# Block-sparse attention with a gated convolution FFN: the sixth head pair's queries and keys are transposed by the DMA crossbar instead of TensorE, with a new instruction order

## The chip, the cores and the metric

The kernel runs on one core of a Trainium2 chip. A core has TensorE (matrix products, results in PSUM), VectorE and ScalarE (elementwise work), GpSimd (here it only issues loads and writes a few constants) and SyncE, called SP here (it only issues transfers). All transfers, whoever issues them, are carried by the same 16 DMA engines. The metric is the device time of one execution in microseconds (us); lower is better. Views of the trace give times from the start of the span, which runs from the first to the last instruction of the profiled execution.

## What is computed

Attention over 4 batches of 8 heads, 768 positions and 64 dimensions per head, with a mask in blocks of 32 positions, followed by a feed-forward block with a gate from a convolution of three taps:

```python
scores = (1.0 / np.sqrt(D)) * np.matmul(q, k.transpose(0, 1, 3, 2))
# mask: neighbouring blocks, first and last block of rows and columns, 3 sampled blocks per block row
scores = np.where(mask, scores, -1000000000.0)
attn = softmax(scores)                       # over the last axis
x = np.matmul(attn, v)                       # heads put side by side: (4, 768, 512)
h = np.maximum(x @ w_in, 0.0)                # (4, 768, 1024)
conv_out[s] = sum over k of conv_w[k] * h[s + k - 1]
out = (h * sigmoid(conv_out)) @ w_out        # (4, 768, 512)
```

Inputs and output are float32; the kernel works in bf16 with float32 accumulation.

## The kernel before

**Head pairs.** Two heads make a pair, so there are 16 pairs, numbered 0 to 15, four to a batch; the sixth is pair 5, in the second batch. A pair's queries and keys must lie with the 64 dimensions on partitions for the score products. They do so in a slot `t` of 24 tiles of 128 columns (five slots are used in turn): tiles 0 to 11 hold queries, 12 to 23 keys, and rows 64 to 87 hold the mask, which is added by the same product because the contraction runs over 88 rows.

**Two ways to fill a slot.** `kq_transposes` (L416) is used for pairs below `NPE`. GpSimd loads keys (192 KB) and the first half's queries (96 KB) into `nat`, with a cast to bf16. TensorE transposes them in blocks of 128x128 into a `mix` bank of PSUM: `k_tr` (L458) takes six transposes, `q_half` (L521) three for each half of the queries. VectorE or ScalarE copies the result into the slot: two copies of 64x768 for keys, two of 64x384 for each half of the queries (L331 on VectorE and L327 on ScalarE are the helper that records all such copies). The second half's queries come later, by a load of their own into `nq`. `kq_crossbar` (L552) is used for the pairs from `NPE` on. GpSimd loads keys and, outside the last batch, the queries of both halves in one load of 192 KB. SP issues two DMA transposes (L596), keys then queries, from `nat` into the staging tile `stg`. Two copies of 64x1536 (`stg_cp`, L602) then fill the slot, each waiting for both transposes. For the first five of these pairs SP also issues `m_turn` (L591), a 72 KB copy that lays the mask rows in the order that the crossbar's layout needs.

**Units.** Scores are computed in 144 units of eight 128x128 blocks. A unit is two groups of score products into an `st` tile (L755, `s`), one exponential on ScalarE over 128x1024 (L767, `exp`), and 8 products with the values (L792, `av`). Work goes through segments: the first or second half of the queries of one batch, 18 units each; the last half is cut in two segments of 12 and 6 units. Pair 5 is first needed in unit 40, and its second queries in unit 58.

**The feed-forward part** of a segment runs beside the next segments' attention. VectorE normalizes a pair's result (L702, `norm`). The result is turned so that features lie on partitions: by TensorE for the first and the last two segments, otherwise by a DMA transpose from SP (L711, `x_xb`). Then come the products with `w_in` (L889, `f1`), evictions of `hE` with the rectifier (L909 on ScalarE or L911 on VectorE, `relu`), the convolution on VectorE (L947, L955), tanh on ScalarE (L994), the gate on VectorE (L997, L1002), the products with `w_out` (L824, `f2`), the eviction of the output (L327 or L331, `ev`) and the store (L833).

**The order.** All operations are recorded in a graph of some 1,800 operations and then written out as the text `ORDER` says: two characters name an operation, a letter (V or A) after them its engine where there is a choice, and a digit the buffer that it takes. Each engine executes its own operations in this order, so the text sets the queue of every engine, GpSimd and SP included. Tile's dependency tracking adds the waits. Loads on GpSimd's queue are spaced by `pace`, a copy of one element that waits until an earlier load has landed (L666) or until a certain unit's exponential is done (L407); `SEQ` and `AHEAD` name the loads that are spaced by the first kind and how far apart.

Of the kernel before, what the change touches and what calls it, by code (L numbers as in the profile page):

```python
# [25 lines left out]
1ZV6s16t2sV25U16c4Z1s6u16d2W6x06y6h6i06q2H04U6z06j22bV6C16D2cV6r6v6k6w6E56L05VV6M1m6A6B6l06N36Q16mV6R6F2GV16G6S0
6H06V06I6W6O16P6X46J06T6+16KV6/2Iid17037301b1l74ig0ih7511pie7b1ifV157ciiA3237g07d26U7hiB16Y1x6Zij1iC7i4ik71iD7l1
727miEilAb2o07q07n07riFim1762qVin7s57827y12pV337zioV7707e7f7A3797j7D07EiJ27a22v04V1v7F1iK7k7o7p7I12wV44W7t3907u
iG3502xV2y17J7N04+7O522zV7K04S2J04T2AV3017B17C2KV07G2Zip17P54PiM7S14R1y7Tiq2LV7U47H7+02X1irVi7v07/7L7MiH7Q8017R
8317w847ViL2M17x8527W08802OV89is0iN7X18a381itiI18d1iuV8286iO8e8l02NV87iR08b8c8f5iy08miS36iv17Y8n18q1iU8riz8giP  # L30
8s07Z8v02UV08wiAV8h8o18p8x3iQiw8t1q8A13428BixAcjb08C48F03aV3iT8GiZ38u8y8zj518H5iV8N1i+jciWi/8O8S08i28Dj08P28Tj6
8j3o28E8IiX8U18k8X1j1538Y8J08Q2+V8R8Z08V3e900512/V3U08W91j2iY9812B28+1o9238/99j74Xj34/3l2jdj49a59d03c38K19e31V2
je37V9f1939i13k3bj83x18LjfA39jj9V28M19n0502P19o9k2jk038V949b14919cjl9p49509s1963p2C19t2EV9g9h9u39A03X02DV9BjmV
jh13nji3mV49C13g13d9F1jjV9Gjq09H59ljF09K09L97jG9mjr9M0jH9q9P19QjIja9R29rjn1jJjo3f39vjsV9w09X0jK9YjpV3w3s09D3q9E
a019x29Z39IjN3a19Jjw1jOjxa249ya50a6jQ9N9Oa752Q0jyVaa19S9TjP9+1ab2SAjt19U12RVac1jujR9/af09VjSa3aga43hjvVjC0a8jL
an1ah2a9jTaojV1adaejD9Wap3jMas0atjXaijz1au1jWax1ayjEVaj03taqarjAaz0jYak0aC0jUavaDjBAawjZ9zaAaBaK1aE2k12aLkf0k2j+
kr1k3aP0aQalaM03A2aFkgk4am2ks3IaR13zk53YaU1aGaN1j/aVk6aO3r4aZ0k03L4aaSa+aW4aTkh3D0k73C3J2ktaH1k8a/2b213M3b3aXki
b413jV3iVba0ku3E1kjA2aYbbaIkvV0b0bf1bc33ZkJ01rb1bg3Okx13Bbh2b5bk03vVbl3Nb60bdbm4kybe3uVbp1bikzV00bq3P0kK3Tbr1b72
bx0b8bykM13yV0kNkLA3aJbC1bjkOVbDbz2bnbol91bsbtkA0bu0bE5kBbvbH0bIkCVkG1bJ4lbkH3FbA0labM1bBbNkIAlcbFbR0bO2bS3QkV0
bGkD0kWkEbT5bKkXbLbZ1b9kYkFAdb+kS1bPbQb/1kT3KV13VV3c20l12jgc3bUldkkkl0kUAc40l3c71bwc8kP13HV4B3kQc943GVbV1c0cc0  # L40
4y1c1l2c5lecdck14bkZc6clce3cakm3RV1knl4kRA4cbcp0cm5bW13SVcqkolh3k91400kpA2lj45ka4n2cr1bXcu1cfkb3Wlf4Ck+likccg3/
cn03+kdA3cvk/lE0cw2l5coke4k0lFlH1lkl014e1cz04clGAcAl6cE1ch0cs4DlgctcxlK0bY0cB0llcy48lL4ol7cFlMVlIcG5cCcM0l8cNcD
lJVlB041cO1lCcicR1m50cSlDAlv1m6kwcT3cW0cXlZ2cHcI1lwl+cY44pcPm8cQcUc/1m7d0lmlp04lV2lxm9d104M0d70lqlnlomad84jcVm0
4d4Ed93dc1lrmbcJ2cZdd462c+mclsde24qlyl/d2d3ltV3lzA1dh0didm1cKlAlQ1dndj4d41cLm1da0lRdo0d5lN04mdr0lSVlOkqm2dbdslPV
dz1lT1ludt14fmd0dAdfdgmedklUdB2mfdllW0cjm3lXmglVAdE0dFm4lYAdpdJ1dG4dqdKmhd6mz1duml1dL0mAmmdO0dw2mnmidv1dCdPmodD
dHdIdMdQ5dW1mjmt0mpmumkmq4x4YdNdX42V244dRdSdY3mBd/0mr47V4e0mvdT0mse11e41dUe5mCe65dZ14Ae90mDV14reamweb443Vee1mR1
mxV24s0mSefdxeg2em0d+e24gV3mU0mVmTV194Fe3e7mWAe8ecener1nd1mX1eo1neesedmYnfet5ehm+04hVm/ew0ej14G1ngmZVfexn0Aei0
eB1eCey0epnl0eqeuev4teknnn11eD4na04Ln2nmeJ0n3AaeKdy2noeL1eO1ezeAeEnhePeFnbnpdVeQ5n41ncVeM1eT0n5nieUmEn6Vn70eV4eN
n84Hnt3njeY1eZeRnunqn9AjmF1e+2el4uV4eSf10mGnweG2eWf2nB2mL0myf35eHmMmH4inv4vAeXmNeIf90fanxfb3e/mInk0mOfe1nDf0mJA3
ffnrnCnEfj0mPV2f4fg0mKfkf50o21nsmQo3ny4zV3n/04wo4Vfo1fl2o0nFfpfcfd4NV1fho1AfinJ1f60nzfq1nKop1fw0nAnP0nGoqfxfB1fC  # L50
fy4nHfmfnornLnIfrfD3fsfG0osfHnMfI0otft1nQnNV2nRounSfufL04IV0nTA3fMnV1fN14JVfQ1nUnWf7nY0nXAnZovf81fz1owfRn+AfAo81
fS4oh0fY0fZfvoio50o9f+5ojo6okg11nOg2o7AoaVfEg60g32fFoloe0g7ox1fJfKomfOozoffPoyg80fTfU0gb1onf/ob1oAocogAfV0gcoo
odAgj0gkoBgd1g0g4g5oF2oT0oGoN1gl3g9go1oIgpoCgaoHoOfWgq5oJgeoUfXgfgm1oDgngt0oKgugg1oEgC1gDgrgv2gsoLoMoPoVgE5ghgw
gH0oWgigIoXA1oQgM1gJ1oRV0p304KgNp4gO3oSp5oYp6gxgV0p7A3gy1pc1gzgWg+1p90gX2papdpbV0bg/peAgF1gGh30h05px2gKh4gA1gLpz
pf0gPgBA0pygQgY0h51pggR0pApi1pjphA6pBhc1pkAhdgSgZh1pChh0pF3gT0pl1pGhe2h2h6h7gUVpmh82pHhipnA3po0hm1hj0h9pDhnpppE1
# [57 lines left out]
def kernel(  # L113
# [70 lines left out]
    A = sb.tile([MR, NB], FP32, tag="A", name="A")  # L184
# [684 lines left out]
    for n, (b, g, tok, C, _) in enumerate(SEGS):  # L869
# [4 lines left out]
        w1 = 128 * C  # L874
# [176 lines left out]
```

## Time and profile before

| | before |
|---|---|
| time, median of 3 runs | 207.29 us (207.22 to 207.52) |
| the profiled execution's own time | 207.06 us |
| its span, first to last instruction | 205.2 us |
| granted TensorE clock | 1.00 |
| transfers | 25.40 MB, mean 124 GB/s |

The profile's page gives for each engine the time in which it was busy and the share of the span, then the chain of work that ended last, then groups of equal instructions. In a group's row stand the line of the code, the engine (PE is TensorE matmul, PEld its weight load, DVE is VectorE, ACT is ScalarE, POOL is GpSimd, SP is SyncE), the tiles written and read, shapes, the count, the total busy time and the mean duration of one in ns, and the idle time of the engine before them with what ended it. Busy time of TensorE comes from modelled ends, so a full TensorE is not a TensorE at its peak.

### The profile page before, as it was taken

What the parts mean: (1) busy time and instruction counts of PE and PEld (TensorE: products, weight loads), DVE (VectorE), ACT (ScalarE), POOL (GpSimd) and SP (SyncE); (2) the same over time, 40 slices, a digit from 0 to 9 for tenths busy, and PEclk for the clock granted to TensorE, in tenths of its full rate; (3) what the DMA queues carried; (4) which work ended last, traced back from release to release, by engine and by line L of the source; (5) the groups of instructions that cost most, each with busy time, mean ns of one, the idle gap of its engine ahead of it and who ended that gap; (6) DMA issues with size and microseconds to landing.
All of it is one profiled execution on the core that took longest, in us unless ns stands there. A gap on an engine that the chain in (4) does not pass through costs nothing.

```text
span 205.2 us, 6186 instructions
## 1 busy us (share of the span) xinstructions
PE 198.2 (97%) x2398; PEld 142.9 (70%) x2417; DVE 184.4 (90%) x561; ACT 190.8 (93%) x251; POOL 60.8 (30%) x125
## 2 busy tenths in 40 slices
PE   7899999999999999999999999999999999999992
PEld 5688878876677776776666767766667667787760
DVE  6899889999999999899999999999999839999961
ACT  6999999999999999899999998999999989998931
POOL 8696652900890149021927011000000000000000
PEclk9999999999999999999999999999999999999999
DMA  6999999997599979999998911655122040011205
GB/s 150 151 176 166 152 188 198 152 220 106 78 154 198 195 105 118 201 103 219 150 177 135 255 30 38 80 134 170 33 72 73 19 132 2 3 51 56 102 3 204
DMA packets 51113, 25.40 MB, mean 124 GB/s; under 512 B 36780, under 2 KB 48140, under 8 KB 51084
## 3 DMA queue, kind: packets, MB, share of 16 engines
q0 software_dynamic: 20000, 11.24, 43.7%
q1 hardware_dynamic: 30796, 13.46, 32.5%
q8 instruction: 19, 0.31, 0.7%
q10 hardware_dynamic: 288, 0.30, 0.4%
q14 instruction: 10, 0.08, 0.2%
HBM read 23.09 MB, written 6.29 MB: 143 GB/s over the span
## 4 chain that ended last, share of the span: by engine, by line
PE 61%; ACT 20%; DVE 14%; issue 4%; ACTq 0%
PE st L755 20%; PE mix L824 15%; ACT pt L767 13%; PE mix L889 10%; PE av L792 10%; DVE m L947 4%; DVE t L331 3%; ACT hE L909 3%; DVE m L955 2%; PE av L229 2%; ACT m L994 2%; ACT t L327 1%; DVE hE L911 1%; DVE xtok L702 1%; PE st L824 1%
## 5 line engine op out<-in xcount | busy, mean ns | idle before, releaser
L767 ACT ACTIVATE pt<-st 128x1024 bf16<-128x1024 f32 (+1 forms) x145 | 142.2, 1041 | 2.6 <-PE st L755 1.4
L755 PE MATMUL st<-t 88*128 88x256 bf16 (+2 forms) x600 | 92.7, 267 | 1.1 <-ACT pt L767 0.4
L792 PEld LDWEIGHTS <-pt 128*128 128x128 bf16 x1152 | 56.2, 97 | 15.1 <-ACT pt L767 0.5
L792 PE MATMUL av<-vt,pt 128*128 128x65 bf16 x1152 | 63.5, 193 | 0.1
L755 PEld LDWEIGHTS <-t 88*128 88x128 bf16 x600 | 48.0, 97 | 20.6 <-issue 2.1
L889 PE MATMUL mix<-xT,winb 128*128 128x384 bf16 (+2 forms) x288 | 55.3, 307 | 0.1
L947 DVE TENSOR_SCALAR m<-hE,cw 128x382 bf16<-128x382 bf16 (+2 forms) x192 | 49.0, 314 | 0.9 <-ACT hE L909 0.5
L824 PE MATMUL mix<-woutb,gT 128*128 128x512 bf16 x165 | 46.5, 379 | 0.6
L955 DVE TENSOR_TENSOR m<-m 128x764 bf16<-128x764 bf16 (+2 forms) x64 | 33.7, 532 | 0.4
L889 PEld LDWEIGHTS <-winb 128*128 128x128 bf16 x288 | 23.5, 97 | 7.5 <-issue 0.5
L994 ACT ACTIVATE m<-m 128x764 bf16<-128x764 bf16 (+2 forms) x32 | 27.1, 847 | 0.0
L824 PEld LDWEIGHTS <-gT 128*128 128x128 bf16 x208 | 17.3, 97 | 9.5 <-DVE gT L1002 0.2
L909 ACT ACTIVATE hE<-mix 128x384 bf16<-128x384 f32 (+2 forms) x38 | 19.4, 527 | 0.6 <-PE mix L889 0.3
L702 DVE TENSOR_TENSOR xtok<-av,rcp 128x384 bf16<-128x384 f32 (+2 forms) x36 | 18.2, 505 | 0.4
L1002 DVE TENSOR_TENSOR gT<-m,hE 128x764 bf16<-128x764 bf16 (+3 forms) x36 | 18.0, 505 | 0.3
L238 POOL DMA_DIRECT2D nat<-in_q_dram x23 | 17.1, 746 | 3.7 <-DMA winb<-in_moe_w_in_dram 2.4
L407 POOL COPY pace<-pt 1x1 bf16<-1x1 bf16 x24 | 6.4, 268 | 38.1 <-ACT pt L767 37.8
L911 DVE TENSOR_SCALAR hE<-mix 128x384 bf16<-128x384 f32 x26 | 14.3, 553 | 3.1 <-PE mix L889 2.8
L238 POOL DMA_DIRECT2D nat<-in_k_dram x15 | 10.9, 726 | 16.2 <-DMA stg<-nat 14.1
L238 POOL DMA_DIRECT2D vn<-in_v_dram x16 | 11.9, 746 | 6.8 <-DVE vt L331 5.1
L331 DVE COPY t<-mix 64x384 bf16<-64x384 bf16 (+1 forms) x30 | 12.3, 416 | 0.7 <-ACT t L327 0.2
L997 DVE TENSOR_SCALAR m<-m 128x764 bf16<-128x764 bf16 (+3 forms) x36 | 11.8, 332 | 0.8 <-ACT m L971 0.2
(80 smaller groups left out, 121.4 us busy)
## 6 DMA issues: line engine op xcount, KB each, us to landing
out_dram<-o2s SPq DMA_DIRECT2D x23, 256.0 KB, 3.3
vn<-in_v_dram POOLq DMA_DIRECT2D x16, 192.0 KB, 5.4
nat<-in_k_dram POOLq DMA_DIRECT2D x15, 192.0 KB, 5.2
nat<-in_q_dram POOLq DMA_DIRECT2D x6, 192.0 KB, 6.1
winb<-in_moe_w_in_dram POOLq DMA_DIRECT2D x2, 512.0 KB, 11.0
woutb<-in_moe_w_out_dram POOLq DMA_DIRECT2D x4, 256.0 KB, 8.2
nat<-in_q_dram POOLq DMA_DIRECT2D x9, 96.0 KB, 5.1
nq<-in_q_dram POOLq DMA_DIRECT2D x6, 96.0 KB, 4.8
```

The costliest lines, as they stand in the source:

```text
L238: return op(name, {eng: occ}, lambda e: on(e).dma_start(out=dst(), in_=src), prio, deps, dma=(kind, service), **kw)
L331: nc.vector.tensor_copy(out=dst, in_=src)
L702: nm = op("norm", {"DVE": t_dps(128 * C)}, lambda e: nc.vector.tensor_tensor(out=xtok_t[xk.index][:, 0:C].rearrange("p c h d -> p h c d"), ...
L755: nc.tensor.matmul(out=st[:, 128 * x:128 * (x + n_)], lhsT=t[0:88, 12 + 6 * hh + kc, :], rhs=t[0:88, idx:idx + (n_ - 1) * (2 if P < NPE el ...
L767: nc.scalar.activation(out=pt_t[ptb.index][:, c0:c1], in_=st_t[stb.index][:, c0:c1], func=AF.Exp, bias=0.0, scale=0.125)
L792: nc.tensor.matmul(out=o[:, off:off + 65], lhsT=pt_t[ptb.index][:, 128 * x:128 * x + 128], rhs=V_t[vslot_b[P].index][:, hh, kc, 0:65], sta ...
L824: nc.tensor.matmul(out=acc(), lhsT=gT_t[gb.index][:, ffc, 128 * t:128 * t + 128], rhs=woutb[:, ffc, c0:c1], start=(ffc == 0), stop=(ffc == ...
L889: nc.tensor.matmul(out=mix_t[hb.index][:, w1 * y:w1 * y + w1], lhsT=winb[:, fc, 128 * ffc:128 * ffc + 128], rhs=xT_t[xt_buf[n].index][:, f ...
L909: nc.scalar.activation(out=dst, in_=src, func=AF.Relu, bias=0.0, scale=0.5)
L947: nc.vector.tensor_scalar(out=m_t[cb.index][:, x, y, 0:w], in0=hE_t[heb.index][:, f0 + y, t0 + x:t0 + x + w], scalar1=cw[:, x, f0 + y:f0 + ...
L955: nc.vector.tensor_tensor(out=m[:, a_, :, 0:w], in0=m[:, a_, :, 0:w], in1=m[:, b_, :, 0:w], op=ALU.add)
L994: th = [op("tanh", {"ACT": t_act(2 * w) + 0.04}, lambda e, cb=cb, w=w: nc.scalar.activation(out=m_t[cb.index][:, 0, :, 0:w], in_=m_t[cb.in ...
```

## The change

`NPE` goes from 6 to 5, so pair 5 is filled by `kq_crossbar` instead of `kq_transposes`. Its keys and queries go through a staging tile; its queries of both halves come in one load; its separate load of second-half queries (`nq5`) leaves the sequence of spaced loads. As the mask copy `m_turn` is made for the first five crossbar pairs, it is now made for pairs 5 to 9 instead of 6 to 10. Score products of pair 5 read the slot in the crossbar's layout. The whole `ORDER` is a different one, from its first line on: positions on every queue, the engine of operations that have a choice, and buffer numbers.

```diff
 ORDER = """
-0M0L001c0R010210N0S0O031h041d1i0V1g0P051P3060Q0712V081e0W090a0T11A0b1f1N00c0d0U0e16A1Q1z00X1F11AA02d21H00Y1GA0f
...
+0M0L000R010210T0N0S0O030W040P050V061N00Q070812V091P10a11A0U0b0c0d1Q0e16A1z10X2130f1F01AA01H00Y1GA1g0g0h0i0/V0+A
...
-    NF, NPE = 4, 6
+    NF, NPE = 4, 5
     WHOLE = ()
-    SEQ = "nq0 nq1 nq2 k4 q4 nq3 v4 k5 q5 w0 v5 w1 k6 q6 w2 w3 v6 k7 q7 v7 nq4 nq5"
+    SEQ = "nq0 nq1 nq2 k4 q4 nq3 v4 k5 q5 w0 v5 w1 k6 q6 w2 w3 v6 k7 q7 v7 nq4"
     AHEAD = 4
```

Counted from the two texts, the operations whose number on an engine differs are these (the transposes and copies of pair 5 among them):

| operation | before | after |
|---|---|---|
| `hE` evictions on ScalarE / VectorE | 38 / 26 | 33 / 31 |
| output evictions on ScalarE / VectorE | 15 / 11 | 17 / 9 |
| staged copies on ScalarE / VectorE | 1 / 19 | 0 / 22 |
| copies of keys from PSUM on ScalarE / VectorE | 3 / 11 | 2 / 10 |
| copies of queries from PSUM on ScalarE / VectorE | 3 / 21 | 4 / 16 |
| copies of turned results on ScalarE / VectorE | 5 / 7 | 4 / 8 |
| transposes of keys / queries on TensorE (groups) | 7 / 13 | 6 / 11 |
| crossbar transposes of queries and keys | 20 | 22 |
| loads of second-half queries, spaced | 2 | 1 |
| pace copies | 42 | 41 |

More of the change, by code (lines that the diff above doesn't have):

```diff
@@ L26 @@
[L26 to L55, printed above, removed]
@@ new lines @@
+6P2X26C16Q26T16DV6M4J6U1li616V1i71x1v146Y06Zi8V01i906+3741ia2GV1ibV756N6R7646Siu26W7907aiw2o06X7b26/7e17012L2qV
+7127f2pVic1iv7g0id7j02T0ieVf7k77if07l5ix7r17s72ig7t1iy787317w07cihV2v14X7diz2O17h2wV47i7x2J07m2xV7y32Z07n7B17C
+iC17u0ii12R2y07D47o07v7G02zV7H1y7p7zij7I52AV7L14L4Q7MiA4N7AikVail07N07T0iD7Uim2MV7V17E7Y1inV7Z7F7J7K7+37O810iEiF
+827P17W7Q18352NV86187iGiB1ir03018827X8e0isiK38fiHio1iL2S17/8j17R808g484858kitV89ipiM8l02U8a8o0iqV88p8h0iN8q18t1
+iI8u8i1p8m8n8v54W2+8y0iOj418b28r2B22PV0iP8s8ziJ8w8G136iS08A38H341i+08c8x4P8I1iT8d8L08MiQj5iViU8N08B8Q12/28Ri/2WV
@@ new lines @@
+8S28C1398V0iW318J8W2VV8KiX8O8P8TiR8U9118X4927qiYj6iZj09338D29608E977Sj1j71o9853f4T2YV39b1j2V29c3g28F2j8A18Y8Z940
+9d09532V9g09h992C033V3a39a9i29e3i9l18+03722DVjd18/9m2EAje4Y3D09n4909t0jfV9uja03j035V2jb9v39y1jcV9zjj19A59fjy19D0
+9EjAjg09F09jjz9I13b0389JjhjB9K19k4Mjk4IjiV9o9Q09q19RjlA3hV49p19w3rjC9S29V19x9WjG09Bjp19r9X49C3n13k9G9+0jHjq3s29/
+jDjrVa31a49sjm0jJa059H9LjI9M9T09U9YjEa50jn3cjK3ua809ZjoVa1a2jLa99N0ag1jO2ah3m4a6aa49Ojs1a7jv0jP9Pai2jFal0amjMjw
+jRan0ab3oaq13xad23larjQac1ajakas5jNjtaoaeav0awjuAjxVaf0aD1ax2apjSaEkk1jW0ataF1aujXaI03C3v3k80jYaJjTayazjZaG0kl
@@ new lines @@
+cu1cl4fV0cx1lBkV1cmk/cq48144lzVcycF0lccrcz0cGlD0l0cvlEkplCVcH24icwcAkdlecK1cLkj42l1li1lFAcccB1cC2cM3cP0cIl+3cJ
+lu045l9cQlflvcD3XcU1l/cNcR1cVljlwVcOcElglkcW4m1d00d1m0cSlo0d234dm247d514jlplhm3cTd6lS0cXda0lTd75dbcYlqlVlldc1cZ1
+m4lr464VlUdf1lsA0dgc+d304kdk0dh0dllmV3c/lJ04glKm5dm2lG1lLVlHltlWds1lIAk7dtlXlnlP0m61lQd4d8d949m8du3dx0ddlYlM1m7
+lNlRAdelZdi4ldjlOA4Sdy4v1m9dndo1dz4dC1dp2dDmamm0me2ms1mbmfmtdE0mgdvdH0dImhdwdAmndJ2mcmidBdFdGmddP1mjdQdU0dq4w4r
+mudR1mkdr1dKdLdVmlmodW0dZ13YV2mp3+3ZVdS0d+4xmqA1mv4aV34m0d/3dTmK0dM14bVmLe20mwA3mMV1he34A1e71e8e42dNdXmN041V1mO
@@ new lines @@
+e91mT14c4ymUdYef0mPAeg4G14nek1mVAn61mQ0eh44umR4s2n7e0ele1mSA6e54ze6eaem5eb1eiec0ej4Bep0edeqmW1n8er4eu1ne0mZ0evn9
+mX4Fm+ngmYAeeneC0nfm/AeodOeeeDew2naesetn01nm2n1eE0n30n2VgeH1eIexnbn44oV4no4qeyeF0my1eJ3ez2nheM0eNeAmzn5AnnmAeB
+eO2nu3eR1eSnieGeKeT4mBncmE04CV04EeW0mCA2eL4HV4eX4pVePeQeY5eUf21npeVf3mFnvf44mGnd0eZnwmHnje/2f714tV2f8nqfc0mIA0
+nU1f0f91e+1f5fdf6nxf10nVnkfe2nX0nWVfafh1nYnlnrmDnZVfbfimJfp0nC1fj0nyfqff4DVfgnI0nznsfu1fvfr1fknDntflnJfw4oi1ok
+fm1fz0fAnKfB5ojnAnBfE1fFfs0nEfG2olnLnFomnMA2fJ0nGV0fKonnR0ftfnnSfL1nO1oofonPnTVfR1opnQAfSo10fT3oa3o2nHn+1obmxn/
@@ L61 @@
+hMpx1qf1qbA0pShQ0hRhN2hzq60qq1hx1qrq7pTpFqgpNq8AhhFhGhZ1pUh+qhA7qtpW0h/5pVhO0hA1pXhBV2qi2pYhS1qspZhH1quhPqc1p+A1
+hIqjhTqvhU1i0qkhJ0i1qdhKAhV1qlq00qeAchWq1i22qmhX1i3q2qy0hYAqni41qzq3i5AqwqAr71q4A3r8qBr9Aq5q+0qoqCq/oRrp0qxr11
+r0Ar2p/qpqDrqqG1r40p1r3Ar5qEra1qHrbqU1qIrc2qVrr3rdr6AqFrf1rgrerk0qJrlrh2rA1rm0qWqKriru0qLrjrsrM0rvrnrorBqMrwrtqN
+rCrDrxrEA1qXrFryV3rG1rHrIqYV0rJrNqO0rKVqPqZrLrOqQrPrzqRrQVrRqSA2qT
 """
```

24 lines of the change are left out of this document (15 added, 9 removed).

## The prediction

> **What bounds the kernel now.** I read the page's first lines, then the stages in the windows view, then ScalarE's timeline.
>
> ```profile
> PE 198.2 (97%) x2398; PEld 142.9 (70%) x2417; DVE 184.4 (90%) x561; ACT 190.8 (93%) x251; POOL 60.8 (30%) x125
> ...
> PE 61%; ACT 20%; DVE 14%; issue 4%; ACTq 0%
> ```
>
> Three engines are above 90% busy, and the chain that ended last runs mostly through TensorE. An average over stages does not say which engine a saving must come from, so the next view cuts the span where the limits change (columns: stretch, then busy time of TensorE matmul, weight load, VectorE, ScalarE and GpSimd, clock, DMA share, GB/s).
>
> ```profile
> 7.00:30.00 23.00, 22.38 (x333) 18.05 (x332) 21.02 (x60) 22.81 (x28) 15.81 (x26) 1.00 1.31 167
> 30.00:50.00 20.00, 19.95 (x288) 15.44 (x288) 19.67 (x62) 19.98 (x25) 6.85 (x15) 1.00 1.27 181
> 50.00:100.00 50.00, 49.48 (x616) 35.11 (x620) 47.59 (x136) 49.20 (x61) 22.83 (x44) 1.00 1.07 146
> 100.00:160.00 60.00, 59.63 (x675) 40.92 (x681) 57.40 (x168) 58.66 (x75) 9.02 (x19) 1.00 0.59 111
> 160.00:170.00 10.00, 9.95 (x102) 6.75 (x102) 5.96 (x17) 8.78 (x12) 0.00 (x0) 1.00 0.27 77
> 170.00:188.00 18.00, 17.89 (x232) 13.74 (x232) 17.49 (x66) 18.00 (x28) 0.00 (x0) 1.00 0.05 17
> 188.00:205.20 17.20, 13.26 (x130) 8.84 (x131) 10.57 (x42) 8.42 (x21) 0.00 (x0) 1.00 0.30 108
> ```
>
> From 7 to 30 us ScalarE is full (22.81 of 23.00) and TensorE has 0.62 us to spare. From 30 to 50 all three are full. From 50 to 170 TensorE is fullest; between 160 and 170 ScalarE idles 1.22 us behind it. From 170 ScalarE is full, with VectorE close behind (17.49 of 18.00), and the last stretch has room everywhere. The clock is 1.00 throughout. So the early stage pays for ScalarE time, the middle for TensorE time, and the end for VectorE time.
>
> What an operation costs on a full engine is the spacing of starts, not its duration, since neighbours overlap. ScalarE's timeline (start, length, count) gives it:
>
> ```profile
> 46.63 0.52 ACT L909 ACTIVATE hE<-mix 128x384 bf16<-128x384 f32 x1
> 47.00 1.98 ACT L767 ACTIVATE pt<-st 128x1024 bf16<-128x1024 f32 x2
> ...
> 55.74 0.65 ACT L327 COPY o2s<-mix 128x512 f32<-128x512 f32 x1
> 56.20 6.87 ACT L767 ACTIVATE pt<-st 128x1024 bf16<-128x1024 f32 x7
> ...
> 138.81 1.47 ACT L327 COPY t<-stg 64x1536 bf16<-64x1536 bf16 x1
> 140.19 1.01 ACT L767 ACTIVATE pt<-st 128x1024 bf16<-128x1024 f32 x1
> ```
>
> An hE eviction costs 47.00 - 46.63 = 0.37 us, an exponential, one per unit of the work, 6.87 / 7 = 0.98 at the pace of that stage, an output eviction 56.20 - 55.74 = 0.46, a staged copy 140.19 - 138.81 = 1.38.
>
> **The change part by part.** Pair 5 (the sixth) loses one k_tr of six transposes and two q_tr of three.
>
> ```profile
> 8.15 0.50 PE L458 MATMUL mix<-ident,nat 128*128 128x128 bf16 x6
> ```
>
> ```profile
> L458 PE MATMUL mix<-ident,nat 128*128 128x128 bf16 x30 | 2.5, 219 | 0.0
> ```
>
> Six take 0.50 us with a last one of 0.219, so the spacing is (0.50 - 0.219) / 5 = 0.056, and twelve give **-0.67 us** of TensorE. (The first row is the timeline's, the second the group's: busy us, mean ns.) The group's busy time bounds the gain from above, 12 x 2.5 / 30 = 1.0. All lie between 30 and 60 us, where TensorE is full, so I count -0.67.
>
> VectorE loses two copies of 64x768 and four of 64x384, and gains two of 64x1536:
>
> ```profile
> L331 DVE COPY t<-stg 64x1536 bf16<-64x1536 bf16 x19 | 10.9, 575 | 0.3
> ...
> L331 DVE COPY t<-mix 64x384 bf16<-64x384 bf16 x20 | 7.0, 349 | 0.6 <-ACT t L327 0.2
> ...
> L331 DVE COPY t<-mix 64x768 bf16<-64x768 bf16 x10 | 5.5, 552 | 0.1
> ```
>
> That is 2 x 0.55 + 4 x 0.35 = 2.5 us out and 2 x 0.575 = 1.15 in: -1.35. The new order spends it. Counting engine letters in both orders, hE evictions on ScalarE go from 38 to 33 (VectorE 26 to 31), output evictions from 15 to 17 (VectorE 11 to 9), staged copies from 1 to 0 (VectorE 19 to 22, two of them pair 5's); a few small copies change sides. ScalarE: -5 x 0.37 - 1.38 + 2 x 0.46 = **-2.3 us**. VectorE's saving is used up by the five evictions and the extra staged copy that it takes over.
>
> Where these fall decides. By the 28th exponential the new order has put two hE evictions fewer on ScalarE: -0.74 us in the stage that ScalarE sets; TensorE's spare 0.62 there just covers it. I count **-0.7**. The rest of ScalarE's relief, 1.6 us, lies where TensorE is full; I count it at nothing (its bounds: 0 and -1.6, and the windows put it nearer 0). Behind the last exponential the new order leaves VectorE one more pair of multiplications, one more output eviction and one small copy less:
>
> ```profile
> L947 DVE TENSOR_SCALAR m<-hE,cw 128x256 bf16<-128x256 bf16 x24 | 5.2, 279 | 0.2 <-ACT hE L909 0.2
> ...
> L331 DVE COPY xT<-mix 128x128 bf16<-128x128 bf16 x1 | 0.2, 206 | 0.0
> ```
>
> The eviction comes when VectorE has room (10.57 of 17.20), so it is counted at nothing; 2 x 0.279 - 0.206 = 0.35, and I count **+0.3** (bounds 0, if TensorE sets the end, and 0.56, if the copy was free).
>
> GpSimd loses one queries load and one pace; the fifth slot's mask copy goes from pair 10 to pair 5, so SP's number of them stays. SP gains two crossbar transposes, which it issues for
>
> ```profile
> L596 SPq DMA_TRANSPOSE stg<-nat x20: 1210/1248/2997, 18.7 to 135.8; - x20
> ```
>
> 1.25 us each (minimum, median, maximum in ns), and the DMA engines gain two transfers of 192 KB while these are loaded most (DMA shares of 1.31 and 1.27 above, 0.59 later).
>
> What hides them is lead: pair 5's load stands near unit 15 in the new order, its copies near units 33 and 36, its first scores at unit 40. The wait that is added is the staged copy's for both transposes; queued behind it on VectorE stand hE evictions, and behind those TensorE's f1, which needs the mix banks. I count 0 here. Without that lead each microsecond of lateness costs one, since VectorE is full from 30 to 50 us; the same two transfers also hold up what is queued behind them on SP, and that is rival C.
>
> Sum: -0.67 - 0.7 + 0.3 = -1.1. The profiled execution took 207.06 us (span 205.2, 1.86 around it), 0.23 under the median of 207.29. So 207.06 - 1.1 = 205.96 profiled, and **206.2** as a median.
>
> On the price of a turn, the Trainium skill (VectorE: DVE Perf Modes, The three transpose paths) gives 390 ns for a 128x128 bf16 transpose on TensorE and 1309 ns by the crossbar. By it the twelve would free 4.7 us, an estimate from that page; the trace disagrees, 0.056 us apiece in a row of six, so the sum does not use it.
>
> **The rivals.** What this kernel's timing can tell from no change is about 0.2%, 0.41 us.
>
> *A, ScalarE's relief is paid in full.* If TensorE's fullness is only waiting for ScalarE, all -2.3 us count, 205.0; with -0.3 from the small copies 204.7. For it: ScalarE is full from 30 to 50. Against: it idles behind TensorE at 160 to 170, and the chain is 61% TensorE.
>
> *B, no change to measure.* TensorE sets the pace from the start of its full stages, the early 0.7 is waited away again, and -0.67 + 0.3 = -0.4 is left: 206.9. For it: 59.63 of 60.00.
>
> *C, slower: SP's queue.* In the new order SP holds pair 7's queries transpose, and behind it the second segment's transposes of head pairs 1 and 2, which stood ahead of it before. That queries load stands behind a pace that waits for the last quarter of w_out. The rows:
>
> ```profile
> 39.54 0.71 POOL L238 DMA_DIRECT2D woutb<-in_moe_w_out_dram  x1
> ```
>
> ```profile
> 56.44 0.48 PE L889 MATMUL mix<-xT,winb 128*128 128x384 bf16 x2
> ```
>
> ```profile
> nat<-in_q_dram POOLq DMA_DIRECT2D x6, 192.0 KB, 6.1
> ...
> woutb<-in_moe_w_out_dram POOLq DMA_DIRECT2D x4, 256.0 KB, 8.2
> ...
> xT<-xtok SPq DMA_TRANSPOSE x24, 3.4
> ```
>
> ```profile
> vn<-in_v_dram POOLq DMA_DIRECT2D x1, 192.0 KB, 3.4
> ...
> xT<-xtok SPq DMA_TRANSPOSE x1, 2.4
> ```
>
> ```profile
> xT<-xtok SPq DMA_TRANSPOSE x3, 5.8
> ```
>
> (Two timeline rows; then DMA rows with the median time to landing, of the whole run, of 50.2 to 54 us, and of 15 to 50 us.) One unit earlier than now, w_out is issued at 38.5 and lands at 46.7. The load then lands at 52.8 by the median, at 50.1 in a quiet queue. Two issues of 1.25 us pass on SP before the last transpose starts, which lands 3.4 or 2.4 later: at 58.7 or 55.0. TensorE wants it one unit (0.98 us) later than now, at 57.4. By medians it waits **1.3 us**; with a quiet queue not at all; it decides from a load that lands after 57.4 - 3.4 - 2.5 = 51.5. The early 0.7 is then lost too: -0.67 + 0.3 + 1.3 = +0.9, **208.2**. For it: the loaded DMA engines up to 50 us. Against: the short landings of 50.2 to 54. With a landing midway between 2.4 and the 5.8 us of the loaded stretch, 4.1, the wait is 2.0 and the time 208.9; with 5.8 whole, 3.7 and 210.6, which the quiet rows make the unlikely end. The Trainium skill speaks on this side: VectorE: DVE Perf Modes, Rules for kernel authors, sends a 128x128 transpose to TensorE wherever a PSUM destination will do, and to the crossbar otherwise; the trace agrees so far that the turn is cheap on TensorE (0.056 us) and slow to land by DMA (3.4 us).
>
> That the change doesn't do what it says is no rival of its own: the turn itself is worth 0.67 us, and everything else is the order, which is in the sum.
>
> **How the numbers follow.** Forecast 0.40 (206.2, its own range 205.6 to 206.8), A 0.07, B 0.17, C 0.36. Faster is forecast and A, 0.47; the same is B, 0.17; slower is C, 0.36. The range goes from A's 204.7 to C's 208.9; beyond are waits longer than priced.
>
> **What would show it.** Twelve fewer L458 and L521 matmuls, 33 hE evictions on ScalarE, and a 28th exponential about 0.7 us earlier show the gains. A ScalarE group idle for more than now before L767, released by TensorE, shows B. TensorE waiting for xT just before the first L889 near 57 us shows C. A VectorE wait for stg near 40 us, or a longer stretch behind the last exponential, would make the prediction wrong by a step that I priced at nothing or at 0.3.

## The result, and the profile after

The kernel after takes 210.22 us (median of 4 runs, 208.97 to 211.0) against 207.41 us: 1.0116 of before, with an interval of 1.0076 to 1.0157. It is slower, where 206.2 us was forecast; the time lies outside the range. The profiled execution took 211.0 us with a span of 209.1, 3.9 more than before's 205.2. Ratios leave out executions of a slower state (over 1.5% above the fastest of their kernel); two profiled executions fell into it, that of the first experiment, at a clock of 0.757, whose page is not used, and that of the late doubled key in experiment 5, at 1.00, which is named where it is used.

The page of the kernel after, its span, the engines and the chain:

```profile
span 209.1 us, 6174 instructions
...
PE 200.2 (96%) x2405; PEld 142.7 (68%) x2405; DVE 185.4 (89%) x562; ACT 189.3 (91%) x246; POOL 61.4 (29%) x123
...
PE 49%; DVE 27%; DMA 11%; ACT 7%; issue 3%; POOL 1%; SPq 0%; DVEq 0%; ACTq 0%
```

The chain of before had no DMA in it; now 11% of it are transfers, and VectorE's share has doubled. The same stages as in the prediction, in the windows view:

```profile
7.00:30.00 23.00, 22.31 (x333) 17.81 (x331) 20.29 (x58) 22.32 (x27) 15.57 (x29) 1.00 1.20 162
30.00:50.00 20.00, 18.94 (x271) 14.55 (x270) 18.10 (x53) 18.64 (x21) 4.88 (x10) 1.00 1.40 158
50.00:100.00 50.00, 48.69 (x609) 34.40 (x606) 47.41 (x139) 47.76 (x57) 20.82 (x42) 1.00 1.03 143
...
188.00:209.20 21.20, 16.99 (x176) 11.37 (x174) 14.78 (x59) 11.29 (x25) 0.00 (x0) 0.97 0.28 101
```

Between 30 and 50 us all three engines were full before; now each idles 1 to 2 us there (18.94, 18.10 and 18.64 of 20.00), so each of them waits for something. What they wait for from 8 to 62 us (the view of waits; total, times, longest):

```profile
PE st L755 <- ACT pt L767: 1.9, 4, 0.8
...
DVE t L331 <- ACT t L327: 1.4, 1, 1.4
DVE t L331 <- DMA stg<-nat: 1.2, 1, 1.2
...
PE mix L889 <- DMA xT<-xtok: 0.3, 1, 0.3
```

None of these rows stands in the same view of before. VectorE's timeline shows where its two waits lie. At the start:

```profile
8.34 0.56 DVE L331 CAST t<-av 64x384 bf16<-64x384 f32 x1 [1.35 <-ACT t L327]
...
9.84 0.95 DVE L331 COPY t<-t 24x3072 bf16<-24x3072 bf16 x1
10.82 0.55 DVE L331 COPY t<-mix 64x768 bf16<-64x768 bf16 x1
```

VectorE's copy of the second head's keys waits 1.35 us for ScalarE's, which the new order puts between the two halves of the first exponential; the copy of the mask rows (24x3072) and pair 1's keys follow behind. (Two small copies of mask rows also change engines and are missing from the table of the change: `m_q1` goes from ScalarE to VectorE, and `m_r1` from VectorE to ScalarE, where it takes 0.51 us at 8.83, ahead of the second unit's exponential.) And near 40 us:

```profile
40.31 0.56 DVE L947 TENSOR_SCALAR m<-hE,cw 128x382 bf16<-128x382 bf16 x2
42.12 0.55 DVE L331 COPY t<-stg 64x1536 bf16<-64x1536 bf16 x1 [1.24 <-DMA stg<-nat]
```

That is pair 5's first staged copy. The chain of work that ended last (start, length) runs here through the load of its queries and their transpose:

```profile
23.57 7.56 DMA nat<-in_q_dram
...
31.19 10.83 DMA stg<-nat
```

Issued at 31.19, the transpose lands at 42.02, and the copy starts at 42.12. A way to read such losses is to lay the exponentials of two traces side by side, one per unit. Start of the nth exponential, in us; columns behind the first are the difference from before ("start", "early5" and "both+q7" are the first, second and last kernels of experiment 2, "turn, early" is the first of experiment 4, "evictions" that of experiment 3):

```
 nth  before  after  start  early5  both+q7  turn, early  evictions
   7    12.7  +1.27  +0.18   +0.88    +0.25        +0.01      +0.44
  28    33.1  +1.19   0.00   +0.59    +0.07        -0.01      +0.60
  37    42.9  +0.41  -0.77   -0.18    -0.70         0.00      -0.20
  43    49.5  +2.42  -0.32   +0.26    -0.08        +0.37      +0.47
  49    56.2  +2.87  +1.23   +0.43    +0.09        +3.68      +0.61
  55    62.1  +3.43  +1.51   +0.71    +0.37        +3.69      +0.88
 115   140.2  +3.18  +1.29   +0.48    +0.13        +3.06      +0.38
 145   186.6  +3.46  +1.16   +0.36    +0.08        +2.78      +0.25
```

After is 1.3 us late by the 7th and 3.4 by the 55th; later stages only shift work about. (The dip of some 0.7 at the 37th, in every kernel with the new order, is a tanh that this order has one unit later.) Each column is one profiled execution, so differences of a few tenths need care: the first exponential already lies between 0.34 us earlier and 0.22 later than before's.

### The profile page after: what moved, and what is told of

Its sections match the earlier page's. It is cut to its first block, busy times and chain, and to the rows that moved or that the text cites. A ratio compares the mean times of both kernels' runs of the same rounds, so it can differ in the third digit from the quotient of the medians.

```text
span 209.1 us, 6174 instructions
## 1 busy us (share of the span) xinstructions
PE 200.2 (96%) x2405; PEld 142.7 (68%) x2405; DVE 185.4 (89%) x562; ACT 189.3 (91%) x246; POOL 61.4 (29%) x123
## 4 chain that ended last, share of the span: by engine, by line
PE 49%; DVE 27%; DMA 11%; ACT 7%; issue 3%; POOL 1%; SPq 0%; DVEq 0%; ACTq 0%
PE st L755 14%; PE mix L824 13%; PE mix L889 11%; DVE m L947 7%; PE av L792 7%; ACT pt L767 5%; DMA stg<-nat 5%; DVE m L955 5%; DVE t L331 4%; DMA nat<-in_q_dram 4%; DVE hE L911 3%; DVE xtok L702 2%; DMA o2s<-in_q_dram 2%; DVE gT L1002 2%; DVE m L997 1%
## 5 line engine op out<-in xcount | busy, mean ns | idle before, releaser
L792 PEld LDWEIGHTS <-pt 128*128 128x128 bf16 x1152 | 57.3, 97 | 16.7 <-DVE vt L331 0.4
L792 PE MATMUL av<-vt,pt 128*128 128x65 bf16 x1152 | 64.8, 193 | 0.1
L947 DVE TENSOR_SCALAR m<-hE,cw 128x382 bf16<-128x382 bf16 (+2 forms) x192 | 50.9, 322 | 1.5 <-ACT hE L909 1.4
L824 PE MATMUL mix<-woutb,gT 128*128 128x512 bf16 x184 | 49.8, 379 | 0.3 <-DVE gT L1002 0.2
L911 DVE TENSOR_SCALAR hE<-mix 128x384 bf16<-128x384 f32 x31 | 17.2, 554 | 5.7 <-ACT pt L767 3.1
L407 POOL COPY pace<-pt 1x1 bf16<-1x1 bf16 x24 | 8.7, 360 | 40.8 <-ACT pt L767 40.6
L909 ACT ACTIVATE hE<-mix 128x384 bf16<-128x384 f32 (+2 forms) x33 | 15.8, 509 | 0.9 <-PE mix L889 0.9
L331 DVE COPY t<-stg 64x1536 bf16<-64x1536 bf16 x22 | 12.8, 586 | 2.1 <-DMA stg<-nat 1.8
L327 ACT COPY o2s<-mix 128x512 f32<-128x512 f32 x16 | 9.5, 593 | 4.5 <-PE mix L824 4.4
```

The costliest lines, as they stand in the source:

```text
L792: nc.tensor.matmul(out=o[:, off:off + 65], lhsT=pt_t[ptb.index][:, 128 * x:128 * x + 128], rhs=V_t[vslot_b[P].index][:, hh, kc, 0:65], sta ...
L824: nc.tensor.matmul(out=acc(), lhsT=gT_t[gb.index][:, ffc, 128 * t:128 * t + 128], rhs=woutb[:, ffc, c0:c1], start=(ffc == 0), stop=(ffc == ...
L911: nc.vector.tensor_scalar(out=dst, in0=src, scalar1=0.5, scalar2=0.0, op0=ALU.mult, op1=ALU.max)
L947: nc.vector.tensor_scalar(out=m_t[cb.index][:, x, y, 0:w], in0=hE_t[heb.index][:, f0 + y, t0 + x:t0 + x + w], scalar1=cw[:, x, f0 + y:f0 + ...
```

## The experiments

Each is compared with runs of before on the same chip; ratios are to before. Edits of the order are given as moves, with the unit near which an operation stands.

**1. Each half of the change alone.** The crossbar for pair 5 in the old order:

```diff
 order of before, pair 5 (NPE = 5)
-GpSimd: keys 17, queries 22, second queries 48; pair 6: keys 8, queries 17
+GpSimd: keys 8, queries 17;                     pair 6: keys 17, queries 22
+SP: xb keys 13, xb queries 26, m_turn 31;  pair 6: xb 30, 31;  pair 7: xb 38, 40
-TensorE: k_tr, q_tr, q_tr;  VectorE/ScalarE: 2 k_cp, 4 q_cp
+VectorE: 2 stg_cp at 35, 36
```

> The order of before, with only what the change itself asks for: the sixth pair's keys and queries come by the crossbar (its loads take the places that the seventh pair's had, its two transposes are issued near units 13 and 26, its staged copies stand where the two evictions of its queries stood), and its TensorE transposes, its four evictions and the second load of its queries are gone. If the loss lies in the new order (theory O), this is 206.2 to 207.2 us: the twelve transposes' 0.67 us or less, and nothing lost. If the loss lies in turning this pair by the crossbar (theory X: late transposes, more load on VectorE and the queues), it is slower than before, 208.3 us or more.

Measured: 1.012 (1.0073 to 1.0168). And the new order with pair 5 on TensorE:

```diff
 order of after, pair 5 (NPE = 6)
-SP: xb, xb, m_turn;  VectorE: 2 stg_cp
+TensorE: k_tr 32, q_tr 34, q_tr 57;  VectorE/ScalarE: 2 k_cp, 4 q_cp;  GpSimd: second queries 48
```

> The order of after, but the sixth pair is turned on TensorE as before (its twelve transposes, its four evictions, its second load of queries put back near units 32 to 36, 44 and 57, and no crossbar transposes for it). Theory O: this is as slow as after or slower by the transposes' own 0.7 us, 210 to 211 us. Theory X: it comes back towards before, 207.3 to 208.5 us.

Measured: 1.012 (1.0078 to 1.0162). Neither theory alone survives: each half costs as much as both. Part of each is my own placing: experiment 4 gets the first down to 1.005 by issuing one load and its transpose earlier, and in the second, between the 31st and the 34th exponential, 1.0 us was lost where TensorE's inserted transposes waited 0.6 us for a bank. The second's start is clean evidence: +1.05 us at the 7th exponential, without any crossbar turn of pair 5.

**2. The two places repaired.**

```diff
 order of after
-all engines, up to the sixth exponential: as after
+all engines, up to the sixth exponential: as before
```

> The kernel after, with the first five exponentials' worth of instructions on all engines in the order of before (the loads' order on GpSimd, ScalarE's and VectorE's setup copies, the first scores). In after the fourth exponential began 1.29 us later than in before. If lateness at the start is carried to the end (theory S, a part of O), this is 1.0 to 1.3 us under after, near 209.0 us. If the cores catch up later because something else is late too (pair 5's staged copies near 41 us), it is within 0.4 us of after.

Measured: 1.0085 (1.0055 to 1.0114), 209.54 us. The start is back (column "start"), but from the 43rd to the 49th exponential 1.55 us go again, with VectorE waiting 1.4 us for a staged tile.

```diff
 order of after, pair 5
-GpSimd: keys 15, queries 20 (nat 2);   SP: xb 19, 26
+GpSimd: keys 11, queries 11 (nat 0);   SP: xb 18, 21
```

> The kernel after, with the sixth pair's loads issued right behind the fifth pair's (unit 11 instead of units 15 and 20, in a staging buffer that is free from the start) and its crossbar transposes issued near units 18 and 21. In after its queries' transpose landed at 42.0 us and the lateness of the exponentials grew from 1.1 to 2.2 us between units 33 and 36. If that wait costs what it shows (theory X, or the part of it that is a late transpose), this is about 1.1 us under after, near 209.1 us; if what bounds 42 to 59 us is VectorE's work itself (theory V), it is within 0.4 us of after.

Measured: 1.0076 (1.0044 to 1.0107), 208.90 us. VectorE's waits from 30 to 62 us in this kernel are one row, and it is not the staged tile:

```profile
DVE hE L911 <- PE mix L889: 1.2, 3, 0.6
```

The loss between 37th and 55th falls from 3.0 us to 0.9. Both together:

```diff
 order of after
+start as in before
+pair 5's loads as above
```

> The kernel after with both repairs: the first five exponentials' instructions in the order of before, and the sixth pair's loads right behind the fifth pair's. If the two losses are separate and each is carried to the end (theory S+L: start, and late transposes), this is after less 1.1 us and less 1.3 to 2 us: 207.2 to 207.8 us, level with before. If TensorE's time is lost elsewhere in the new order as well, it stays at or above 208.5 us.

Measured: 1.0024 (0.999 to 1.0058): level with before. The two losses are separate, and both were carried to the end. The median, 208.35 us, missed the 207.2 to 207.8 that I expected; the profiled run, with 209.97 the longest, shows one reason, a staged tile:

```profile
DVE t L331 <- DMA stg<-nat: 1.7, 1, 1.7
PE st L755 <- DVE t L331: 1.6, 1, 1.6
```

I took it for pair 7's and issued that pair's queries earlier. It is pair 6's: SP issued the transpose of pair 6's queries at 47.25, it landed at 53.23 in the chain of this execution, and pair 7's was issued at 52.16.

```diff
 order of the kernel above, pair 7's queries
-GpSimd: 41, behind the last quarter of w_out
+GpSimd: 30, ahead of it
```

> The kernel after with the start of before and the sixth pair's loads early (208.35 us median, with a wait of 1.7 us for pair 7's staged tile in its profile), and now pair 7's queries' load issued at unit 30, ahead of the last quarter of w_out, instead of at unit 41 behind it. Theory D+L: the wait for pair 7's staged tile goes, and the time is 206.8 to 207.8 us, level with before or a little under. If that wait was a mere accident of one run: 208.0 to 208.5 us, unchanged.

Measured: 1.0024 (0.9997 to 1.0051), 208.17 us. In its profile the wait is gone and the exponentials of the table are at most 0.37 us behind before up to the 55th, but the time is the same within the interval, as the expectation has it for a wait that was an accident of one run. This is the best version with the change, and it does not beat before.

**3. Is it VectorE's extra evictions?**

```diff
 both repairs; hE evictions of units 24, 27, 39
-VectorE (L911)
+ScalarE (L909)
```

> As the first kernel of this call (both repairs), with the three gate evictions of units 24, 27 and 39 that the new order moved to VectorE given back to ScalarE. Theory V (the loss of 42 to 59 us is VectorE's extra evictions): 0.5 to 1 us faster than the first. If ScalarE is what bounds the first 40 us: 0.3 to 0.8 us slower, three evictions of 0.8 us less what ScalarE's gaps take up.

Measured: 1.0040 (1.0006 to 1.0073), 208.31 us against 208.35: no difference that can be measured, where this theory had 0.5 to 1 us. The theory that VectorE's evictions make the loss falls, and so does the worth of relieving ScalarE of three.

**4. The old order again, with the loads early.**

```diff
 order of before, pair 5 by the crossbar
-GpSimd: queries 17, behind the second half of w_in;  SP: xb queries 26
+GpSimd: queries 15, ahead of it;                     SP: xb queries 20
```

> The order of before with the sixth pair by the crossbar, as in the first of these experiments, but its queries' load is issued ahead of the second quarter of w_in (unit 15 instead of 17) and its transpose ahead of unit 20. Theory L (what costs is that transposes land after the staged copies' turn on VectorE): 206.4 to 208.0 us, since pair 5's are then early. Theory D (what costs is that the DMA engines are full from 10 to 53 us, so that two more transposes make all later ones land later, pair 7's too): still 209 us or more, with VectorE waiting for pair 7's or pair 6's staged tile near 45 to 53 us.

Measured: 1.005 (1.0005 to 1.0096), against 1.012. Its trace is the clearest: with nine of the twelve transposes gone the exponentials keep step with before to 0.02 us from the 5th to the 37th; by the 46th 0.34 us are lost, and 3.34 more by the 49th. VectorE's wait between 48 and 60 us, then the windows (the column before the last two is the clock):

```profile
DVE t L331 <- DMA stg<-nat: 2.0, 2, 1.7
```

```profile
52.00:54.00 2.00, 0.74 (x12) 0.43 (x10) 0.58 (x2) 2.00 (x3) 1.63 (x4) 1.00 1.37 129
54.00:56.00 2.00, 1.41 (x14) 0.96 (x15) 1.97 (x6) 0.70 (x2) 1.94 (x5) 0.79 1.29 247
56.00:58.00 2.00, 2.00 (x9) 0.88 (x7) 1.70 (x6) 0.71 (x1) 1.56 (x4) 0.50 1.37 224
58.00:60.00 2.00, 2.00 (x17) 1.16 (x15) 0.60 (x2) 1.61 (x3) 2.00 (x5) 0.86 1.27 177
```

TensorE idles 1.26 + 0.59 = 1.85 us in one piece, and then the clock is low: 2 x (0.21 + 0.50 + 0.14) = 1.7 us of TensorE time. Together 3.55. The tile is pair 6's. In the chain the transpose of its queries, issued at 38.31, takes 15 us:

```profile
38.31 14.99 DMA stg<-nat
```

It landed at 53.30; the expectations below call the tile pair 7's, and the last of them has it land at 57 us. Nor does every execution lose this much: three of the ten runs took 207.8 us, level with before (207.74 in this comparison), and the other seven 209.2 to 212.7. Even the three gain nothing from the transposes that TensorE no longer makes.

Three attempts to make this order fit failed. All were meant for pair 7, though they also issue the transpose of pair 6's queries 2 to 3 us earlier.

```diff
 order of the kernel above
+a third staging tile; pair 7: xb 31, 33;  pair 6: xb 27, 29
+GpSimd: pair 7's queries ahead of the third quarter of w_out
```

> The order of before with the sixth pair by the crossbar and its loads early, as in the kernel that kept step with before to 0.00 us up to the 37th exponential and then lost 3.7 us where VectorE waited 1.7 us for pair 7's staged tile; here a third staging buffer lets pair 7's transposes be issued near units 31 and 33 instead of 38 and 40, and its queries' load stands ahead of the third quarter of w_out. Theory D+L (the added transposes push pair 7's past its turn): the wait for the staged tile goes or shrinks under 0.5 us and the time is 206.6 to 208.0 us. If the DMA engines are simply full until 55 us and the order of issue only deals out the lateness: another tile is late by as much, 208.5 us or more.

Measured: 1.0429 (1.0393 to 1.0466). Pair 5's mask rows now stood behind the stalled transposes on SP, and TensorE waited for them:

```profile
PE st L755 <- DMA t<-mback: 7.1, 1, 7.1
```

```diff
 order of the kernel above
+SP by due time: m_turn 24, 28, 33 ahead of pairs 6 and 7; xT transposes behind pair 7
-GpSimd: pair 7's values 30
+GpSimd: pair 7's values 36
```

> A candidate that should beat both if the queue theory holds: the order of before with the sixth pair by the crossbar, its loads early, a third staging buffer, and SyncE's queue in the order of what is due (pair 5, its mask rows, pair 6, pair 7, then the xT transposes, which aren't read before 56 us); the eighth pair's values are loaded behind the last quarter of w_out. Theory Q: no wait for staged tiles or mask rows between 40 and 58 us, and 206.6 to 207.6 us, the twelve transposes' 0.67 us less at best. Theory D: some tile is late at 47 to 56 us all the same, 208.5 us or more, with a clock of 0.5 to 0.8 behind the stall.

Measured: 1.0394 (1.0349 to 1.0439); it was my edit, since VectorE copies those values early in this order:

```profile
DVE vt L331 <- DMA vn<-in_v_dram: 6.1, 1, 6.1
```

```diff
 order of the kernel above, two staging tiles
-GpSimd: pair 7's values 36;  VectorE: their copy 41
+GpSimd: pair 7's values 41;  VectorE: their copy 49
```

> The order of before with the sixth pair by the crossbar, two staging buffers as in after, its mask rows and the transposes of pairs 5, 6 and 7 ahead of the xT transposes in SyncE's queue, pair 7's queries' load ahead of the third quarter of w_out, and pair 7's values with their copy on VectorE eight units later, so that their bytes aren't ahead of the transposes. In the kernel that kept step with before up to the 37th exponential, VectorE waited 1.7 us for pair 7's staged tile, which landed at 57 us. If the transposes can be made to land in time in this order: no such wait, and 206.6 to 207.6 us, under before. If the stretch up to 55 us can't take the two transposes: a wait of 1.5 us or more for a staged tile or for an xT tile, a clock of 0.5 to 0.8 behind it, and 209 us or more.  The copy of the values on VectorE is checked by its own wait: if it waits for them, the two cases can't be told apart.

Measured: 1.0156 (1.0104 to 1.0208). In its profile (209.13 us, the shortest run) the wait for a staged tile is 0.2 us, but an xT tile, a vector result behind it and the last staged copies are each up to 0.9 us late, and other runs show clocks of 0.982. No arrangement that I tried made room in this order.

**5. What a transpose more costs.** Before, with transposes issued a second time into a tile that nothing reads; nothing else is changed:

```diff
         def turned(e, x):
             nc.sync.dma_start_transpose(out=stg..., in_=nat_t[nb.index][:, x])
+            if P == 6:
+                nc.sync.dma_start_transpose(out=spare[:, x]..., in_=nat_t[nb.index][:, x])
```

> The kernel before, with its order untouched, but each of the seventh pair's two crossbar transposes is issued a second time into a tile that nothing reads; it adds two transposes to the queues between 18 and 45 us and takes nothing away. Theory D: 0.5 to 2 us slower than before, with later transposes landing 1 us or more later and VectorE waiting for staged tiles. Theory L: nothing that can be measured, 207.2 to 207.9 us, since nobody waits for them.

Measured: 1.0057 (1.0027 to 1.0087). Two transposes that take part in nothing cost 1.2 us. SP's timeline here, and then in before:

```profile
38.92 4.87 SPq L597 DMA_TRANSPOSE stg<-nat  x2
43.84 2.94 SPq L600 DMA_TRANSPOSE spare<-nat  x1
...
49.11 2.69 SPq L597 DMA_TRANSPOSE stg<-nat  x1
```

```profile
36.18 4.30 SPq L596 DMA_TRANSPOSE stg<-nat  x2
...
42.89 1.27 SPq L596 DMA_TRANSPOSE stg<-nat  x1
```

The last one of these, of pair 7's queries, is issued 6.2 us later. Not all of that is SP's queue: the first row, pair 7's keys, already starts 2.7 us later, behind the load of these keys, which took 11.1 us to land. With the control `if P == 14:`, in a stretch with a third of the DMA load:

> The control for the doubled transposes: the kernel before with the fifteenth pair's two transposes issued twice, in 124 to 131 us, where the DMA share is 0.43 and not 1.3. Theory D (the price is that of a full DMA stretch): nothing that can be measured, 207.2 to 207.9 us. If a transpose costs by itself, wherever it stands: 1.2 us, as the doubled ones of the seventh pair did.

Measured: 1.0159 (1.0111 to 1.0207). Both theories had this wrong. Up to 140 us it keeps step with before (+0.27 us at the 115th exponential); then an xT transpose that stands behind the doubled one is issued 1.5 us later (SP's timeline here and in before) and lands 4.0 us after that, TensorE waits for it, and the clock falls (waits and windows of this kernel). In before TensorE read this tile without a wait 2.6 us after its issue, so later issue and longer landing both have a part in the wait.

```profile
141.47 1.21 SPq L717 DMA_TRANSPOSE xT<-xtok  x1
```

```profile
139.95 1.21 SPq L711 DMA_TRANSPOSE xT<-xtok  x1
```

```profile
PE mix L895 <- DMA xT<-xtok: 2.7, 1, 2.7
```

```profile
146.00:148.00 2.00, 2.00 (x25) 1.53 (x23) 2.00 (x8) 1.22 (x2) 0.00 (x0) 0.71 0.31 102
148.00:150.00 2.00, 2.00 (x7) 0.84 (x6) 2.00 (x8) 0.91 (x2) 0.00 (x0) 0.50 0.00 0
150.00:152.00 2.00, 2.00 (x26) 1.29 (x25) 1.26 (x3) 1.14 (x2) 0.00 (x0) 0.94 0.00 0
```

2.7 us of wait and 2 x (0.29 + 0.50 + 0.06) = 1.7 of clock make 4.4; the 121st exponential is 4.65 - 0.27 = 4.4 later. To part the queue from the load, one doubled transpose where SP has nothing behind it, in the quiet stretch (`if P == 14 and x == 1:`) and in the full one (`if P == 6 and x == 1:`):

> The kernel before with only the key transpose of the fifteenth pair issued twice (near 126 us), where SyncE's queue has nothing else until 129 us. In the kernel that doubled the queries' transpose too, the exponentials kept step with before (+0.27 us) up to 140 us, and then TensorE waited 2.7 us for an xT transpose that SyncE had issued 1.5 us later. Theory Q (the price is the place in SyncE's queue: what is issued behind it is late by its issue time, and the loss is what that has not to spare): 0, 207.0 to 208.0 us. If a transpose costs by itself: 0.6 us or more.

Measured: 1.0001 (0.9972 to 1.003).

> The kernel before with only the key transpose of the seventh pair issued twice (near 21 us), where the DMA share is 1.34 and SyncE's queue is free until 34 us: the DMA engines get the load, the queue has nothing behind it. Theory Q: under 0.3 us, 207.2 to 208.1 us. Theory D (full DMA engines make everything later): half of the 1.2 us of the two doubled ones or more, 208.0 us and up.

Measured: 1.0009 (0.9978 to 1.0041), 208.04 us. Neither shows a cost for one transpose more where nothing that is soon waited for stands behind it on SP (the mask copy `mback`, which does stand behind the early one, is issued 3.4 us later and nobody waits for it); the intervals still allow 0.3 and 0.4%. That the cost is the place in SP's queue fits all four kernels, but it is not parted from the load, since the two that were slower have two transposes more and these have one.

The profiled execution of the late doubled key, the longest of its ten (210.14 us), calls for care. The same xT transpose is issued at 141.22, only 0.4 us later than before when the exponentials' own lateness of 0.89 is taken off, and lands 4.6 us later; TensorE waits for it as in the kernel with both doubled:

```profile
PE mix L895 <- DMA xT<-xtok: 2.4, 1, 2.4
```

Two of the 23 runs of before in that comparison took as long (210.15 and 211.53 us). They have no profile, so it stays open whether the doubled key had a part in this wait.

The transfers don't settle it either. The windows of 50 to 55 us of before, of after, and of the kernel with the late doubled key, whose instructions up to 120 us are before's (last two columns: DMA share, GB/s):

```profile
50.00:55.00 5.00, 4.80 (x60) 3.14 (x60) 4.90 (x15) 5.00 (x7) 3.23 (x7) 1.00 0.31 45
```

```profile
50.00:55.00 5.00, 4.29 (x58) 3.01 (x55) 4.94 (x16) 4.49 (x5) 2.51 (x6) 1.00 1.04 129
```

```profile
50.00:55.00 5.00, 4.89 (x61) 3.21 (x60) 4.90 (x15) 5.00 (x7) 3.17 (x7) 1.00 1.01 94
```

Before had worked off its transfers by 50 us and after had not; but the third had not either, and its exponentials kept step with before to 0.04 us there. How full the transfers are in one execution does not show what the change adds.

## Why the prediction was wrong, step by step

**The step that failed is the fourth, pair 5's staged copies, whose wait for the two transposes was counted at 0.** The prediction named the condition ("without that lead each microsecond of lateness costs one") and did not check the lead: from a load near unit 15 to a copy near unit 33 it looked long. Unit 15 is that of the keys' load; the queries' stands near unit 20. In the trace it was issued at 23.57 us and took 7.56 to land, the transpose was issued at 31.19 and took 10.83, and the copy, whose turn came at 40.88, waited 1.24. The prediction itself showed 1.31 and 1.27 as DMA shares there, and took a lead in units for a lead in time. Issuing the loads earlier takes the ratio from 1.0116 to 1.0076, and with the start repaired from 1.0085 to 1.0024: 0.4 to 0.6%, 0.8 to 1.3 us. The intervals within each of these pairs overlap, so the single repairs rest on their traces (the loss from the 37th to the 55th exponential falls from 3.0 to 0.9 us); both repairs together are clear of after.

**A term was missing: the start.** The new order was read for which engine gets what, not for the first ten microseconds, and the sum has no term for them. Going back to before's start takes 1.0116 to 1.0085, or 1.0076 to 1.0024: 0.3 to 0.5%. Which part of it costs most, the order of GpSimd's first loads or ScalarE's copies between the first exponentials, was not tried apart.

**Step 1, twelve transposes at -0.67 us: worth nothing where they stood.** Nine of them were gone by the 37th exponential of the kernel in experiment 4, and it came 0.00 us earlier. The windows of before and of that kernel suggest why:

```profile
30.00:40.00 10.00, 10.00 (x161) 8.17 (x160) 9.73 (x29) 9.98 (x13) 5.71 (x13) 1.00 1.44 193
```

```profile
30.00:40.00 10.00, 9.65 (x155) 7.82 (x154) 8.95 (x27) 9.97 (x13) 4.77 (x13) 1.00 1.42 186
```

Without the nine transposes TensorE has 0.35 us to spare, and ScalarE is busy 9.97 of 10, as it was in before (9.98); before's full TensorE, 10.00, had been read as one that sets the pace. Rival B, which counts the same 0.67, falls with it; rival A, which pays ScalarE's relief in full, falls by the result and by experiment 3, where three evictions changed nothing.

**Step 2, a 28th exponential 0.7 us earlier: it came 1.2 later**, with both repairs 0.39 later, and with pair 7's earlier load too 0.07. Giving three evictions back to ScalarE changed nothing (experiment 3). The group rows show that the engine letters were counted rightly, 33 on ScalarE and 31 on VectorE:

```profile
L911 DVE TENSOR_SCALAR hE<-mix 128x384 bf16<-128x384 f32 x31 | 17.2, 554 | 5.7 <-ACT pt L767 3.1
...
L909 ACT ACTIVATE hE<-mix 128x384 bf16<-128x384 f32 (+2 forms) x33 | 15.8, 509 | 0.9 <-PE mix L889 0.9
```

**Step 3, +0.3 behind the last exponential: not shown.** From the last exponential's start to the end it is 209.1 - 190.1 = 19.0 us against 205.2 - 186.6 = 18.6, which looks right. But the same stretch varies by as much with the order unchanged: it is 18.5 to 19.3 us in the kernels that keep before's order there (experiments 4 and 5), and 18.6 in the second of experiment 1, which keeps after's. The chain there runs through TensorE in after from 186 to 205 us; in before it ran through VectorE up to 193.9.

**Rival C had the sign and the queue, not the tile.** TensorE waited 0.3 us for xT, not 1.3; everything else was some 3 us late by then, which would hide such a wait. Its mechanism, a transpose on SP that pushes a later one past its turn, fits the doubled transposes, with 2.7 us of wait for xT; in after, the wait was for a staged tile. That the unlikely end of its prices, 210.6, lies near the measured 210.2 is luck, since it stood for a wait of 3.7 us for xT.

## What to carry to other kernels

Work that leaves TensorE's list for a DMA joins another list: before pricing the DMA at nothing, write down when its input lands, what the landing takes in that stretch, and when its reader's turn comes, in microseconds, for it and for everything behind it on its queue. Time saved on an engine counts only where that engine is the one others wait for; laying the exponentials of two traces side by side shows where it is lost. A wait names a tile, not a pair: find the transfer that filled it before moving another. And of a new order the first ten microseconds deserve a reading of their own.

## What the runs showed of the hardware

A stall of TensorE can cost more than its idle time. After idle pieces of 1.85 us (experiment 4) and 2.7 us (both late transposes doubled) the granted clock fell to 0.50 and took 1.7 us more in each case. The length of the idle piece alone doesn't decide it: the wait of 1.6 us in the kernel with both repairs left the clock at 1.00 (windows of that kernel, where the piece is cut in two at 54 us), and so did the wait of 2.4 us in the kernel with the late doubled key:

```profile
52.00:54.00 2.00, 1.35 (x33) 1.14 (x30) 0.65 (x2) 0.73 (x1) 0.12 (x1) 1.00 1.32 205
54.00:56.00 2.00, 1.02 (x7) 0.58 (x8) 1.97 (x5) 1.50 (x2) 0.00 (x0) 1.00 1.01 149
```

```profile
144.00:146.00 2.00, 0.18 (x2) 0.11 (x2) 0.00 (x0) 1.25 (x2) 0.00 (x0) 1.00 0.34 124
146.00:148.00 2.00, 2.00 (x28) 1.41 (x27) 1.75 (x6) 0.94 (x2) 0.00 (x0) 1.00 0.24 74
```

After the wait of 7.1 us in the kernel with three staging tiles the clock stayed low for longer, at 0.50 to 0.55 in every window from 50 to 60 us.

The Trainium skill (TensorE: Matmul & The Clock Gate, What's actually happening) says that the clock is halved after an idle window of about 3.4 us and restored after a busy one of as much; half of 3.4 is 1.7, an estimate from that page. The two stalls of 1.85 and 2.7 us agree with the 1.7, but the fall came after less idle time than one such window.

Two crossbar transposes of 192 KB more took more packet time than their bytes suggest. The queue rows of before and of the kernel with the seventh pair's two transposes doubled (packets, MB, share of 16 engines' span):

```profile
q1 hardware_dynamic: 30796, 13.46, 32.5%
```

```profile
q1 hardware_dynamic: 32396, 13.86, 35.5%
```

That is 0.355 x 207.1 - 0.325 x 205.2 = 6.8 us of all sixteen engines' packet time for 0.4 MB, which at before's mean of this queue would be 2.0 us. The size is not settled by these profiles: the same difference is 5.4 and 6.9 us in the two kernels with one doubled transpose, and 3.8 to 8.7 us in the kernels with pair 5's two.

SP can be held as well. The six issues of 18 to 60 us in the kernel of experiment 4 (minimum, median, maximum in ns):

```profile
L596 SPq DMA_TRANSPOSE stg<-nat x6: 1281/2826/4014, 19.0 to 50.5; - x6
```

Before's four in that stretch took 1210/1368/2997 and after's six 1222/1293/4178: each kernel has an issue of 3 us or more there, while the median of the whole run before was 1.25. The Trainium skill (DMA: Bandwidth & Descriptors, Rules for kernel authors) says that transfers issued from different engines share the same sixteen DMA engines and interleave. That both queues carry packets at once fits (589 of GpSimd's and 364 of SP's from 36 to 38 us of before); that one slows the other no run here isolates.
